# An expert's first weight matrix: its magnitude from ScalarE's sums of squares instead of VectorE's largest absolute values

## The chip, the core and the metric

The kernel runs on one core of a Trainium2 chip. The metric is the device time of one launch in microseconds (us), the median of three runs. The engines named below are PE (TensorE, the matmuls), PEld (its weight loads), DVE (VectorE), ACT (ScalarE), POOL (GpSimd) and SP (SyncE, which here only issues transfers).

## The reference, cut to what matters

Attention through 32 packed queries gives x, 4608 tokens of 512 numbers. A mixture of eight experts with top-1 routing follows, then a dense layer. All is float32.

```python
expert_idx = np.argmax(x @ w_gate, axis=1)
for e in range(E):                          # E = 8, w1: 512 x 1024, w2: 1024 x 512
    xe = x[expert_idx == e]
    h = np.maximum(xe @ w1[e], 0.0)
    out[expert_idx == e] = gate_w * (h @ w2[e])
...
h = out @ w_in                              # 512 x 2048
r = np.maximum(h, 0.0)
return (s * (r * r) + b) @ w_out            # 2048 x 512
```

## The kernel before

The kernel sorts the tokens by expert into tiles of 128 tokens. Attention and the first expert tiles come first. From tile 11 on (`FIRST`) the expert tiles and the dense layer are interleaved, and that is the stage that this text is about: tiles 11 to 38, from about 325 us to 1215 us of the span. After it the dense layer runs alone.

In that stage a float32 operand is split into two float16 parts, high and low, and a product is made of three matmuls (high by high, low by high, high by low). To split the weights of a tile, `wscale` finds one scale for the whole matrix, and `wsplit` writes the high part with ACT (`wh`, L885) and the low part with DVE (`wl`, L887), in four chunks of 128 x 1024. Part 0 is the first matrix w1, part 1 the second one w2. The scale needs a magnitude of the matrix, which is found chunk by chunk: for part 0 by `big1`, a DVE reduction of the largest absolute value (L845), for part 1 by `big2`, an ACT square whose sum goes to an accumulator (L854). `wscale` then takes the largest of the four (L860), exchanges it between the partitions on POOL (L862), and works the scale out in a few tiny DVE instructions.

`slot(i, ...)` is one step of the stage. An even slot (tile 11, 13, ...) runs the eight column blocks of the dense layer's first product (`mlp_1`, four before and four after the second product of the previous tile, `moe_2s`), and then the first product of its own tile (`moe_1s`). An odd slot has the two halves of the dense layer's second product (`mlp_2`) in their place. Two slots thus handle two expert tiles and 256 tokens of the dense layer.

The preparation of weights stands in one queue of generators, `wq`, in the order scale, split, load of the next tile's part, magnitude of the next part: `wscale(i,0)`, `wsplit(i,0)`, `wload(i+1,0)`, `big2(i)`, `wscale(i,1)`, `wsplit(i,1)`, `wload(i+1,1)`, `big1(i+1)`. `tick(n)`, called between groups of matmuls, takes the next n steps from `wq` and then one step of each chain in `chains` (`xsplit` for the tokens of the next tile, `moe_y` for the results of the last, `gate`). Each engine works through its own instructions in the order in which the program issues them, so an instruction of `wq` that waits holds up all that its engine has behind it. All the magnitudes of part 0 of tiles 12 to 38 fall into odd slots.

`wload` issues four transfers of 512 KB on SP, each conditional on a change of expert (`chg`), and each after the split of the old contents of its chunk. `xsplit` ends with a transposing transfer on the same SP queue, `xTs`, which `moe_1s` of the tile reads. In `mlp_1`, ACT frees a block of PSUM (`r`, L976); there are two such blocks (`gp`), so the third group of matmuls waits for the first one's `r`.

Of the kernel before, what the change touches and what calls it, by code (L numbers as in the profile page):

```python
# [11 lines left out]
F32 = mybir.dt.float32  # L12
F16 = mybir.dt.float16
I32 = mybir.dt.int32
BF16 = mybir.dt.bfloat16
AF = mybir.ActivationFunctionType
ALU = mybir.AluOpType
AX = mybir.AxisListType
# [3 lines left out]
FIRST = 11  # L22
# [85 lines left out]
SURE = NMT - 4  # L108
# [38 lines left out]
def attn_moe_mlp_kernel(ctx, tc, q, k, v, p, w_gate, w1, w2, w_in, w_out, s_, b_, cst_d, csh_d, out):  # L147
    nc = tc.nc
    V, A, T, G, SY = nc.vector, nc.scalar, nc.tensor, nc.gpsimd, nc.sync
# [5 lines left out]
    def flat(t):  # L155
        return t.rearrange("p a b -> p (a b)")
# [23 lines left out]
    st = {}  # L180
# [3 lines left out]
    wf = [[wp.tile([128, 4, 256], F32, name=f"wf1{c}") for c in range(4)],  # L184
          [wp.tile([128, 2, 512], F32, name=f"wf2{c}") for c in range(4)]]

    def wload(i, part):
        src = (w1, w2)[part]
        if part == 0:
            st["er", i] = (SY.value_load(eid[0:1, i:i + 1], min_val=0, max_val=E - 1),  # L190
                           SY.value_load(chg[0:1, i:i + 1], min_val=0, max_val=1) if i else None)
        e, ch = st["er", i]
        sl, cond = src[ds(e, 1)].rearrange("o c p f -> (o c) p f"), dict(cond=ch) if i else {}
        for c in range(4):
            SY.dma_start(out=flat(wf[part][c]), in_=sl[c], **cond)

    io = ctx.enter_context(tc.tile_pool(name="io", bufs=2))
# [328 lines left out]
    def gather(i):  # L526
        x = io.tile([128, XW], F32, tag="x", name="xg", bufs=3)
        G.indirect_dma_start(out=x, out_offset=None, in_=xd if i >= EARLY else xd[0:128 * KNOWN, :], in_offset=bass.IndirectOffsetOnAxis(ap=rho[:, i:i + 1] if i >= EARLY else rho0[:, i:i + 1], axis=0))
        st["x", i] = x

    def moe_x(i, ps):
        x = st["x", i]
        st["xp", i] = pt = ps.tile([128, 4, 128], F32, tag="t", name="ptx")
        for c in range(4):
            T.transpose(pt[:, c, :], x[:, 128 * c:128 * c + 128], ident)

    def moe_xc(i):
        xT = io.tile([128, 4, 128], F32, tag="xT", name="xT")
        A.copy(out=xT, in_=st.pop(("xp", i)))
        st["xT", i] = xT  # L540

    def gate(i):

        lg = st["x", i][:, DM:DM + E]
        nm = io.tile([128, 1], F32, tag="nm", name="nm")
        V.tensor_reduce(out=nm, in_=lg, axis=AX.X, op=ALU.max, negate=True)
        yield
        ex = io.tile([128, E], F32, tag="ex", name="ex")
        f = io.tile([128, 1], F32, tag="f", name="f")
        A.activation(out=ex, in_=lg, func=AF.Exp, bias=nm, accum_out=f)  # L550
        st["f", i] = f
# [252 lines left out]
    io2 = ctx.enter_context(tc.tile_pool(name="io2", bufs=2))  # L804
# [6 lines left out]
    def moe_1(i):  # L811
        xT = st.pop(("xT", i))
        hT = io.tile([128, 8, 128], F32, tag="hT", name="hT")
        for c in range(4):
            if c % 2 == 0:
                hp = ps_h.tile([128, 4, 128], F32, tag="h", name="hp")
            for m in range(2):
                for kk in range(4):
                    T.matmul(hp[:, 2 * (c % 2) + m, :], wf[0][c][:, kk, 128 * m:128 * m + 128], xT[:, kk, :], start=kk == 0, stop=kk == 3)
            if c % 2:  # L820
                A.activation(out=hT[:, 2 * c - 2:2 * c + 2, :], in_=hp, func=AF.Relu)
            tick(FW[0])
        st["hT", i] = hT
# [12 lines left out]
    def pow2(s, a, mul):  # L836
        V.tensor_scalar(out=s, in0=a, scalar1=1e-30, scalar2=mul, op0=ALU.max, op1=ALU.mult)
        V.tensor_scalar(out=s.bitcast(I32), in0=s.bitcast(I32), scalar1=0x7F800000, scalar2=None, op0=ALU.bitwise_and)

    def big1(i):  # L840

        am = io.tile([128, 4], F32, tag="am1", name="am1")
        st["am1", i] = am
        for c in range(4):
            V.tensor_reduce(out=am[:, c:c + 1], in_=wf[0][c], axis=AX.XY, op=ALU.max, apply_absolute_value=True)  # L845
            yield

    def big2(i):

        am = mp.tile([128, 4], F32, tag="am2", name="am2")  # L850
        st["am2", i] = am
        for c in range(4):
            jk = mp.tile([128, 2, 512], F16, tag="jk2", name="jk2", bufs=1)
            A.activation(out=jk, in_=wf[1][c], func=AF.Square, accum_out=am[:, c:c + 1])  # L854
            yield

    def wscale(i, part):
        am = st.pop((f"am{part + 1}", i))
        m = mp.tile([128, 1], F32, tag=f"wm{part}", name="wm")
        V.tensor_reduce(out=m, in_=am, axis=AX.X, op=ALU.max)  # L860
        pm = mp.tile([128, 1], F32, tag=f"wp{part}", name="wp")
        G.partition_all_reduce(pm, m, 128, bass_isa.ReduceOp.max)  # L862
        yield
        s = mp.tile([128, 1], F32, tag=f"ws{part}", name="ws")
        r = mp.tile([128, 1], F32, tag=f"wr{part}", name="wr")
        if part == 0:
            pow2(s, pm, 0.25)
            V.reciprocal(out=r, in_=s)  # L868
        else:
            V.tensor_scalar(out=s, in0=pm, scalar1=1e-30, scalar2=None, op0=ALU.max)  # L870
            V.tensor_scalar(out=s.bitcast(I32), in0=s.bitcast(I32), scalar1=1, scalar2=0x7F800000,
                            op0=ALU.logical_shift_right, op1=ALU.bitwise_and)
            V.reciprocal(out=r, in_=s)
            V.tensor_scalar(out=r, in0=r, scalar1=2.0 ** -54, scalar2=None, op0=ALU.mult)
            s1 = st["ws", i]
            V.tensor_scalar(out=s, in0=s, scalar1=2.0 ** 54, scalar2=s1, op0=ALU.mult, op1=ALU.mult)
        st["ws", i] = s
        st["wr", i, part] = r
        yield
# [59 lines left out]
    def mlp_load(k):  # L939

        yT = io2.tile([128, 2, 4, 256], F16, tag="yT", name="yT")
        rows = ybuf[256 * k:256 * k + 256, :]
        SY.dma_start_transpose(out=yT.rearrange("p a c t -> p (a c) t"), in_=rows[:, 0:DM].bitcast(F16))
        st["yT", k] = yT
        y = io2.tile([128, 2, 2], F32, tag="yg", name="yg")
        SY.dma_start(out=y, in_=rows[:, DM:DM + 2].rearrange("(t p) c -> p t c", p=128))
        st["y", k] = y

    def mlp_y(k):
        ys = []  # L950
        y = st.pop(("y", k))
        for t in range(2):
            dt = io.tile([128, 1], F32, tag="dt", name="dt", bufs=4)
            V.tensor_tensor(out=dt, in0=y[:, t, 0:1], in1=y[:, t, 0:1], op=ALU.mult)
            tk_ = io.tile([128, 1], I32, tag="tk", name="tk", bufs=4)
            V.tensor_copy(out=tk_, in_=y[:, t, 1:2].bitcast(I32))
            ys.append((dt, tk_))
        st["ys", k] = ys
# [44 lines left out]
    wq = []  # L1003
# [23 lines left out]
    for i in range(1, FIRST):  # L1027
        if i == 1:
            wq.append(cg)
            chains.append(gate(1))  # L1030
        elif i + 1 < FIRST:
            moe_x(i + 1, ps_tr)
            moe_xc(i + 1)
        if i > 1:
            gather(i + 2)
        if i == FIRST - 1:
            mlp_load(0)
        moe_1(i)
        wload(i + 1, 0)
        if i == FIRST - 1:  # L1040
            mlp_y(0)
            chains.append(xsplit(FIRST))
            wq.append(big1(FIRST))
        if i == 1:
            gather(3)
            moe_x(2, ps_tr)
            moe_xc(2)
        moe_2(i)
        wload(i + 1, 1)
        chains.append(gate(i + 1))  # L1050
# [9 lines left out]
                    op0=ALU.logical_shift_right, op1=ALU.bitwise_and)  # L1060
    V.tensor_scalar(out=qm[:, 8:9].bitcast(I32), in0=top[:, 1:2].bitcast(I32), scalar1=1, scalar2=0x7F800000,
                    op0=ALU.logical_shift_right, op1=ALU.bitwise_and)
# [13 lines left out]
    mp = ctx.enter_context(tc.tile_pool(name="mp", bufs=2, side="right"))  # L1076
# [3 lines left out]
    def later(f, *a):  # L1080
        f(*a)
        return
        yield
# [13 lines left out]
    done = {}  # L1097
    i = FIRST
# [17 lines left out]
    def queue1(i):  # L1116
        if i < SURE:
            done[i, 0] = wsplit(i, 0)
            wq.extend([wscale(i, 0), done[i, 0]] + ([later(wload, i + 1, 0)] if i + 1 < SURE else []) + [big2(i)])

    def queue2(i):
        if i < SURE:
            done[i, 1] = wsplit(i, 1)
            wq.extend([wscale(i, 1), done[i, 1]])
            if i + 1 < SURE:
                wq.extend([later(wload, i + 1, 1), big1(i + 1)])

    def slot(i, x1, x2):

# [92 lines left out]
```

## Time and profile before

| what | before |
|---|---|
| median of three runs | 1397.02 us (1391.12 to 1397.62) |
| the profiled execution's own time | 1395.76 us |
| its span, first to last instruction | 1394.0 us |
| PE, PEld busy | 1350.3 us (97%), 934.8 us (67%) |
| DVE, ACT, POOL busy | 1055.7 us (76%), 798.8 us (57%), 187.1 us (13%) |
| mean granted clock of TensorE | 0.992 |

The profile is of one execution. Its own time is 1.8 us above its span, which is what lies around the first and the last instruction. A busy time is a sum over the instructions of an engine; matmuls are pipelined and overlap. An idle time in brackets stands with the engine or transfer that ended it.

### The profile page before, as it was taken

Reading aid. Unit: us, or ns where it says so; the run is one execution under the profiler, and the core shown is the slowest. Engines: PE = TensorE matmul, PEld = TensorE weight load, DVE = VectorE, ACT = ScalarE, POOL = GpSimd, SP = SyncE. Lnnn points to the kernel's source line nnn. Section 1 sums busy time; section 2 is a strip of 40 time slices with the busy share of each in tenths; the row PEclk is TensorE's granted clock in tenths of the full one; section 3 lists DMA queues with packets and bytes.
Section 4 is the critical chain, followed back from the end, with each engine's and each line's share of the span. In section 5 each row is a group of like instructions: output and inputs, shape, how many; then the busy total and the mean of one; then the engine's idle time right before and its main releaser. Section 6 shows DMA issues by size and latency. Waiting matters only on the chain. (4 is left out here: it accounts for less than half of the span.)

```text
span 1394.0 us, 29467 instructions
## 1 busy us (share of the span) xinstructions
PE 1350.3 (97%) x11365; PEld 934.8 (67%) x11365; DVE 1055.7 (76%) x2330; ACT 798.8 (57%) x1314; POOL 187.1 (13%) x283
## 2 busy tenths in 40 slices
PE   7999989999999999999999999899999999999998
PEld 4666766677575857667675857576676858667764
DVE  3777888887798788888888888788888888733322
ACT  3655444455675757677675757577676757523221
POOL 0223211111011010111111110101111110100000
PEclk9999999999999999999999999999999999999999
DMA  9897347462116111141223211611112111111000
GB/s 331 277 364 257 131 173 265 147 204 58 27 40 164 44 40 39 44 155 44 55 92 107 48 45 39 160 35 47 32 48 53 32 46 47 31 27 40 16 16 16
DMA packets 106145, 133.62 MB, mean 96 GB/s; under 512 B 77135, under 2 KB 79311, under 8 KB 102928
## 3 DMA queue, kind: packets, MB, share of 16 engines
q1 hardware_dynamic: 91696, 92.76, 22.6%
q0 software_dynamic: 9120, 29.32, 6.4%
q10 hardware_dynamic: 5184, 9.61, 1.9%
q8 instruction: 91, 1.49, 0.5%
q14 instruction: 54, 0.44, 0.1%
HBM read 216.39 MB, written 29.30 MB: 176 GB/s over the span
## 5 line engine op out<-in xcount | busy, mean ns | idle before, releaser
L971 PE MATMUL gp<-yT,win_h 128*128 128x256 f16 x1152 | 314.6, 273 | 3.6 <-ACT r L976 3.4
L973 PE MATMUL gp<-yT,win_l 128*128 128x256 f16 x1152 | 314.6, 273 | 0.0
L972 PE MATMUL gp<-yT,win_h 128*128 128x256 f16 x1152 | 314.6, 273 | 0.0
L887 DVE SCALAR_TENSOR_TENSOR wl<-wf,wr,wh 128x1024 f16<-128x1024 f32 x224 | 278.3, 1279 | 23.9 <-ACT wh L885 23.8
L885 ACT ACTIVATE wh<-wf,wr 128x1024 f16<-128x1024 f32 x224 | 245.8, 1139 | 59.9 <-DVE wr L868 45.0
L993 PE MATMUL op<-wout_h,g 128*128 128x512 f16 x512 | 194.0, 379 | 0.8 <-DVE osb L999 0.8
L994 PE MATMUL op<-wout_l,g 128*128 128x512 f16 x512 | 194.0, 379 | 0.0
L995 PE MATMUL op<-wout_h,g 128*128 128x512 f16 x512 | 194.0, 379 | 0.0
L976 ACT ACTIVATE r<-gp,cf 128x512 f32<-128x512 f32 x144 | 98.8, 686 | 141.5 <-PE gp L973 141.5
L979 DVE TENSOR_TENSOR r<-r 128x512 f32<-128x512 f32 x144 | 99.7, 692 | 81.1 <-ACT g L978 57.3
L919 PE MATMUL hps<-xTs,wh 128*128 128x128 f16 x896 | 154.4, 221 | 6.1 <-DMA xTs<-xs 5.9
L920 PE MATMUL hps<-xTs,wh 128*128 128x128 f16 x896 | 154.4, 221 | 0.0
L921 PE MATMUL hps<-xTs,wl 128*128 128x128 f16 x896 | 154.4, 221 | 0.0
L845 DVE TENSOR_REDUCE am<-wf 128x1 f32<-128x1024 f32 x112 | 132.0, 1211 | 0.0
L972 PEld LDWEIGHTS <-win_h 128*128 128x128 f16 x1152 | 112.9, 98 | 18.3 <-issue 3.6
L971 PEld LDWEIGHTS <-win_h 128*128 128x128 f16 x1152 | 112.9, 98 | 17.7 <-issue 3.0
L973 PEld LDWEIGHTS <-win_l 128*128 128x128 f16 x1152 | 112.9, 98 | 13.3
L854 ACT ACTIVATE jk<-wf 128x1024 f16<-128x1024 f32 x112 | 118.1, 1054 | 2.6
L924 ACT ACTIVATE hTs<-hps 128x512 f16<-128x512 f32 x56 | 33.4, 597 | 122.0 <-PE hps L921 122.0
L919 PEld LDWEIGHTS <-wh 128*128 128x128 f16 x896 | 88.7, 99 | 9.0 <-issue 6.8
L980 DVE TENSOR_TENSOR g<-r,g 128x512 f16<-128x512 f32 x128 | 88.6, 692 | 4.4
L995 PEld LDWEIGHTS <-g 128*128 128x128 f16 x512 | 50.1, 98 | 60.4
(254 smaller groups left out, 2326.2 us busy)
## 6 DMA issues: line engine op xcount, KB each, us to landing
wf<-in_moe_w_dram SPq DMA_DIRECT2D x304, 512.0 KB
xd<-x ACTq DMA_DIRECT2D x36, 260.5 KB
k<-in_k_dram SPq DMA_DIRECT2D x16, 576.0 KB
v<-in_v_dram SPq DMA_DIRECT2D x16, 512.0 KB
q<-in_q_dram SPq DMA_DIRECT2D x8, 1024.0 KB
raw<-in_moe_w_in_dram SPq DMA_DIRECT2D x8, 1024.0 KB
raw<-in_moe_w_out_dram SPq DMA_DIRECT2D x8, 1024.0 KB
p<-in_p_dram SPq DMA_DIRECT2D x8, 128.0 KB
```

The lines of the kernel that those rows point to most:

```text
L845: V.tensor_reduce(out=am[:, c:c + 1], in_=wf[0][c], axis=AX.XY, op=ALU.max, apply_absolute_value=True)
L885: A.activation(out=wh[part][c], in_=wf[part][c], func=AF.Copy, scale=r)
L887: V.scalar_tensor_tensor(out=wl[part][c - 1], in0=wf[part][c - 1], scalar=r, in1=wh[part][c - 1], op0=ALU.mult, op1=ALU.subtract)
L919: T.matmul(o, h_, xT[:, 0, kk, :], start=kk == 0, stop=False)
L920: T.matmul(o, h_, xT[:, 1, kk, :], start=False, stop=False)
L921: T.matmul(o, l_, xT[:, 0, kk, :], start=False, stop=kk == 3)
L971: T.matmul(hp[:, i, :], h_, yT[:, 0, kk, :], start=kk == 0, stop=False)
L972: T.matmul(hp[:, i, :], h_, yT[:, 1, kk, :], start=False, stop=False)
L973: T.matmul(hp[:, i, :], l_, yT[:, 0, kk, :], start=False, stop=kk == 3)
L993: T.matmul(op, h_, wout_h[:, kf, :], start=kf == 0, stop=False)
L994: T.matmul(op, h_, wout_l[:, kf, :], start=False, stop=False)
L995: T.matmul(op, l_, wout_h[:, kf, :], start=False, stop=kf == 15)
```

## The change

`big1` and `big2` become one function `big(i, part)`, which squares a chunk on ACT and sums it into an accumulator for either part. The 112 DVE reductions of part 0 (28 tiles of four chunks) go, and 112 ACT squares with their accumulator reads come in, at the same places in `wq`. In `wscale`, part 0 gets the form of part 1: five tiny DVE instructions where there were three. The small tiles `am` and the thrown-away squares (`jkw`, one buffer for both parts) come from the pool `io2`, which exists before the first call; `am1`, `am2` and `jk2` go.

```diff
-    def big1(i):
-        am = io.tile([128, 4], F32, tag="am1", name="am1")
-        st["am1", i] = am
+    def big(i, part):
+        am = io2.tile([128, 4], F32, tag=f"am{part}", name="am")
+        st["am", i, part] = am
         for c in range(4):
-            V.tensor_reduce(out=am[:, c:c + 1], in_=wf[0][c], axis=AX.XY, op=ALU.max, apply_absolute_value=True)
+            jk = io2.tile([128, 1024], F16, tag="jkw", name="jkw", bufs=1)
+            A.activation(out=jk, in_=flat(wf[part][c]), func=AF.Square, accum_out=am[:, c:c + 1])
             yield
-    def big2(i):
-        am = mp.tile([128, 4], F32, tag="am2", name="am2")
...
-            jk = mp.tile([128, 2, 512], F16, tag="jk2", name="jk2", bufs=1)
-            A.activation(out=jk, in_=wf[1][c], func=AF.Square, accum_out=am[:, c:c + 1])
...
     def wscale(i, part):
-        am = st.pop((f"am{part + 1}", i))
+        am = st.pop(("am", i, part))
...
+        up = 2.0 ** (54 if part else 59)
+        V.tensor_scalar(out=s, in0=pm, scalar1=1e-30, scalar2=None, op0=ALU.max)
+        V.tensor_scalar(out=s.bitcast(I32), in0=s.bitcast(I32), scalar1=1, scalar2=0x7F800000,
+                        op0=ALU.logical_shift_right, op1=ALU.bitwise_and)
+        V.reciprocal(out=r, in_=s)
+        V.tensor_scalar(out=r, in0=r, scalar1=1.0 / up, scalar2=None, op0=ALU.mult)
         if part == 0:
-            pow2(s, pm, 0.25)
-            V.reciprocal(out=r, in_=s)
+            V.tensor_scalar(out=s, in0=s, scalar1=up, scalar2=None, op0=ALU.mult)
         else:
...
+            V.tensor_scalar(out=s, in0=s, scalar1=up, scalar2=st["ws", i], op0=ALU.mult, op1=ALU.mult)
...
-            wq.append(big1(FIRST))
+            wq.append(big(FIRST, 0))
...
-... + [big2(i)])
+... + [big(i, 1)])
...
-                wq.extend([later(wload, i + 1, 1), big1(i + 1)])
+                wq.extend([later(wload, i + 1, 1), big(i + 1, 0)])
```

## Rows read from the trace of the kernel before

**Rows 1.** Page, part 1: busy us, share of the span, instructions.

```profile
PE 1350.3 (97%) x11365; PEld 934.8 (67%) x11365; DVE 1055.7 (76%) x2330; ACT 798.8 (57%) x1314; POOL 187.1 (13%) x283
```

**Rows 2.** What PE waited for from 300 us on: total us, times, longest.

```profile
PE hps L919 <- DMA xTs<-xs: 5.9, 2, 3.8
PE gp L971 <- ACT r L976: 3.4, 1, 3.4
PE tp L1056 <- DVE dg L738: 1.8, 1, 1.8
```

**Rows 3.** Busy us (count) by engine, granted clock, DMA share, GB/s, per stretch.

```profile
456.00:888.00 432.00, 432.00 (x3590) 298.56 (x3589) 369.42 (x716) 297.70 (x444) 56.36 (x68) 1.00 0.25 66
...
394.00:396.00 2.00, 0.67 (x4) 0.47 (x4) 1.63 (x6) 1.97 (x4) 0.00 (x0) 0.64 0.00 0
396.00:398.00 2.00, 2.00 (x11) 1.40 (x10) 1.97 (x3) 1.97 (x3) 0.00 (x0) 0.51 0.00 0
...
430.00:432.00 2.00, 2.00 (x11) 0.93 (x10) 0.75 (x3) 1.61 (x2) 0.00 (x0) 1.00 0.00 0
```

**Rows 4.** ACT timeline: first hidden activation of five even slots; start, length, idle.

```profile
417.76 0.60 ACT L924 ACTIVATE hTs<-hps 128x512 f16<-128x512 f32 x1 [1.33 <-PE hps L921]
...
484.42 0.60 ACT L924 ACTIVATE hTs<-hps 128x512 f16<-128x512 f32 x1 [1.32 <-PE hps L921]
...
547.18 0.60 ACT L924 ACTIVATE hTs<-hps 128x512 f16<-128x512 f32 x1 [1.33 <-PE hps L921]
...
860.98 0.60 ACT L924 ACTIVATE hTs<-hps 128x512 f16<-128x512 f32 x1 [1.33 <-PE hps L921]
...
929.09 0.60 ACT L924 ACTIVATE hTs<-hps 128x512 f16<-128x512 f32 x1 [1.33 <-PE hps L921]
```

**Rows 5.** Page, part 5: both forms of magnitude; busy us, mean ns.

```profile
L845 DVE TENSOR_REDUCE am<-wf 128x1 f32<-128x1024 f32 x112 | 132.0, 1211 | 0.0
...
L854 ACT ACTIVATE jk<-wf 128x1024 f16<-128x1024 f32 x112 | 118.1, 1054 | 2.6
```

**Rows 6.** DVE timeline of an odd slot: start, length, idle before.

```profile
423.31 2.34 DVE L845 TENSOR_REDUCE am<-wf 128x1 f32<-128x1024 f32 x2
...
429.09 0.16 DVE L860 TENSOR_REDUCE wm<-am 128x1 f32<-128x4 f32 x1
...
439.28 0.16 DVE L860 TENSOR_REDUCE wm<-am 128x1 f32<-128x4 f32 x1 [0.77 <-ACT jk L854]
```

**Rows 7.** ACT timeline of the same odd slot.

```profile
420.93 1.14 ACT L885 ACTIVATE wh<-wf,wr 128x1024 f16<-128x1024 f32 x1
...
430.39 4.27 ACT L885 ACTIVATE wh<-wf,wr 128x1024 f16<-128x1024 f32 x4 [2.81 <-DVE wr L868]
434.56 1.05 ACT L854 ACTIVATE jk<-wf 128x1024 f16<-128x1024 f32 x1
...
440.77 4.27 ACT L885 ACTIVATE wh<-wf,wr 128x1024 f16<-128x1024 f32 x4 [0.94 <-DVE wr L874]
```

**Rows 8.** SP's queue in the same odd slot: issue start, time issuing.

```profile
432.88 0.36 SPq L195 DMA_DIRECT2D wf<-in_moe_w_dram  x1
...
438.23 1.28 SPq L906 DMA_TRANSPOSE xTs<-xs  x1
```

**Rows 9.** ACT timeline where an odd slot goes over into an even one.

```profile
578.44 0.60 ACT L924 ACTIVATE hTs<-hps 128x512 f16<-128x512 f32 x1 [3.12 <-PE hps L921]
582.32 0.60 ACT L924 ACTIVATE hTs<-hps 128x512 f16<-128x512 f32 x1 [3.28 <-PE hps L921]
583.74 0.69 ACT L976 ACTIVATE r<-gp,cf 128x512 f32<-128x512 f32 x1 [0.82 <-PE gp L973]
```

**Rows 10.** ACT timeline of tile 12's odd slot and the even slot behind it.

```profile
369.08 4.27 ACT L885 ACTIVATE wh<-wf,wr 128x1024 f16<-128x1024 f32 x4 [8.40 <-DVE wr L868]
...
393.98 0.72 ACT L900 ACTIVATE xs<-xg,xr 128x512 f16<-128x512 f32 x1 [5.92 <-DVE xr L897]
394.61 0.67 ACT L976 ACTIVATE r<-gp,cf 128x512 f32<-128x512 f32 x1
```

More of the change, by code (lines that the diff above doesn't have):

```diff
@@ L838, in pow2 @@
         V.tensor_scalar(out=s.bitcast(I32), in0=s.bitcast(I32), scalar1=0x7F800000, scalar2=None, op0=ALU.bitwise_and)
-    def big1(i):
-        am = io.tile([128, 4], F32, tag="am1", name="am1")
-        st["am1", i] = am
+    def big(i, part):
+        am = io2.tile([128, 4], F32, tag=f"am{part}", name="am")
+        st["am", i, part] = am
         for c in range(4):
-            V.tensor_reduce(out=am[:, c:c + 1], in_=wf[0][c], axis=AX.XY, op=ALU.max, apply_absolute_value=True)
-            yield
-    def big2(i):
-        am = mp.tile([128, 4], F32, tag="am2", name="am2")
-        st["am2", i] = am
-        for c in range(4):
-            jk = mp.tile([128, 2, 512], F16, tag="jk2", name="jk2", bufs=1)
-            A.activation(out=jk, in_=wf[1][c], func=AF.Square, accum_out=am[:, c:c + 1])
+            jk = io2.tile([128, 1024], F16, tag="jkw", name="jkw", bufs=1)
+            A.activation(out=jk, in_=flat(wf[part][c]), func=AF.Square, accum_out=am[:, c:c + 1])
             yield
     def wscale(i, part):
-        am = st.pop((f"am{part + 1}", i))
+        am = st.pop(("am", i, part))
         m = mp.tile([128, 1], F32, tag=f"wm{part}", name="wm")
@@ L865, in wscale @@
         r = mp.tile([128, 1], F32, tag=f"wr{part}", name="wr")
+        up = 2.0 ** (54 if part else 59)
[4 more added lines that the diff above has]
+        V.tensor_scalar(out=r, in0=r, scalar1=1.0 / up, scalar2=None, op0=ALU.mult)
         if part == 0:
-            pow2(s, pm, 0.25)
-            V.reciprocal(out=r, in_=s)
-        else:
[L870 to L876, printed above, removed]
+            V.tensor_scalar(out=s, in0=s, scalar1=up, scalar2=None, op0=ALU.mult)
+        else:
+            V.tensor_scalar(out=s, in0=s, scalar1=up, scalar2=st["ws", i], op0=ALU.mult, op1=ALU.mult)
         st["ws", i] = s
@@ L1118, in queue1 @@
             done[i, 0] = wsplit(i, 0)
-            wq.extend([wscale(i, 0), done[i, 0]] + ([later(wload, i + 1, 0)] if i + 1 < SURE else []) + [big2(i)])
+            wq.extend([wscale(i, 0), done[i, 0]] + ([later(wload, i + 1, 0)] if i + 1 < SURE else []) + [big(i, 1)])
     def queue2(i):
```

## The prediction

> **What bounds the kernel now.** The page's first part comes first [rows 1]: PE is busy for 97% of the span, DVE for 76%, ACT for 57%. A busy PE says little by itself, so the next view is what PE waited for from 300 us on [rows 2]: twice a transposed token tile `xTs` (5.9 us, of which one wait is 3.8), once an ACT result `r` (3.4 us), once a DVE result before the stage begins (1.8 us). Then the stretches [rows 3], whose columns behind the length are PE, PEld, DVE, ACT and POOL: from 456 to 888 us PE is busy for all of 432 us at full clock, DVE for 369 and ACT for 298. The last check is the rhythm [rows 4]: the same instruction of an even slot comes at 484.42 and at 547.18, so an undisturbed pair of slots takes 62.76 us, with no wait of PE in it.
>
> So neither DVE nor ACT is the bound in an undisturbed pair. Moving work between them is worth nothing there, as long as ACT doesn't become late. What is to be had is in the three disturbed places, and these cost more than their waits. From 417.76 to 484.42 are 66.66 us, 3.90 more than a pair, for a wait of 2.1 (5.9 less 3.8). From 860.98 to 929.09 are 68.11, 5.35 more, for a wait of 3.8. The third place, the wait for `r` near 394, shows why: behind it the granted clock is 0.64 and 0.51 for two stretches of 2 us [rows 3], that is, in part the lower of its two levels, 1.2 GHz in place of 2.4. PE had idled for 3.4 us before it fell. In these stretches 0.67 us of work at 0.64 and 2.00 us at 0.51 lose 0.24 + 0.98 = 1.2 us, so this place costs 3.4 + 1.2 = 4.6 us.
>
> The Trainium skill (Trainium Kernel Development and Optimization, the paragraph on reading a trace under Performance Expectations) says that matmul busy time misjudges how near a kernel is to its limit and that weight-load busy time is one of the better measures. By that rule PE, with loads busy for 67%, could have room of up to a third, and freeing DVE would pay in every pair. The constant 62.76 us without a wait shows no such room that a faster DVE could fill.
>
> **What goes and comes, in instructions.** 112 reductions of 1.211 us leave DVE, and 112 squares of 1.054 us come to ACT [rows 5]. The busy sum of DVE falls by 132 us, that of ACT rises by 118 us and 112 accumulator reads. Off the path this is free.
>
> ScalarE: Activation LUTs, Rules for kernel authors, in the Trainium skill, speaks against the move: maxima and products belong on VectorE, which it calls up to about three times as fast per element in 16 bit. By that rule a chunk on ACT would cost up to 3 x 1.21 = 3.6 us; the trace disagrees for these float32 chunks, with 1.05 against 1.21. I go by the rows.
>
> **The odd slot.** Here the reductions stand between the end of one split and the start of the next, and they are in series with it. In the slot around 430 us [rows 6, 7], ACT ends the last high part of w2 at 420.93 + 1.14 = 422.07. DVE ends its low part and starts reducing at 423.31, the token chain `xsplit` comes between the reductions, and the largest of the four is taken at 429.09. ACT starts the next split at 430.39, after an idle 2.81.
>
> After the change ACT can square at once from 422.07. What four squares with their reads cost up to the same reduction is seen with part 1 (w2) of the same slot: from 434.56 to 439.28, 4.72 us. So the reduction comes at 426.79. From there to the split's start were 1.30 us for part 0 (429.09 to 430.39); with the longer `wscale` it is what part 1 needs, 439.28 to 440.77, 1.49 us. The split starts at 428.28 in place of 430.39, 2.1 us sooner, and all that hangs on it in this slot comes sooner too: low parts, loads, `xTs`, the second magnitude, the second split. The two more tiny instructions are in this sum (0.19 us). The POOL exchange is unchanged. The squares need w1 loaded, as the reductions did, and these never waited for it (idle 0.0 [rows 5]); behind a square that did wait, ACT's hidden activations and every `r` would be queued.
>
> **The three places.**
> *Near 448.* `xTs` is issued at 438.23 behind four loads of w1, the first of them at 432.88, and each of these waits for a low part of the split [rows 8]. The transfer engines are idle just before (share 0.00 from 430 to 432 [rows 3]), so the whole train should move 2.1 us forward. The wait is 2.1 us. I take it as gone, clock loss and all: 3.9 us. Bounds: 0, if the transposing transfer is held up by something that doesn't move, and 3.9.
> *Near 893.* Same train, wait 3.8 us, so 1.7 remain, and I let the clock loss stay: a gain of 2.1 us. Bounds: 0, and 5.35 - 1.7 = 3.7 if the shorter wait no longer lowers the clock.
> *Near 394.* Tile 12's split starts at 369.08, after ACT idled 8.40 us for the DVE scale, and the lag runs on: ACT is held at `xs` until 393.98 (idle 5.92, on DVE's `xr`), `r` comes only at 394.61, and PE stands [rows 10]. DVE is late because it does the last two reductions before `xr`. In the new kernel the split starts 2.1 us sooner, ACT does the next four squares where it idled 5.92, and DVE comes to `xr` without reductions. The late `r` ended at 394.61 + 0.67 = 395.28, and PE had waited 3.4 us, so it is needed by 391.9. What brings it forward is 2.1 us of the earlier split, and of the rest of the 5.92 that ACT idled for `xr` some two reductions of 1.21, which DVE no longer has in front of it: 2.1 + 2.4 = 4.5 us, against 3.4 needed, while the squares take 4.72 of ACT, which fit into the 5.92. No wait, but a margin of a microsecond or less. I take the full 4.6 us; bounds 0 and 4.6.
> *Near 324* (1.8 us [rows 2]): DVE's queue is shorter by four reductions, but `xs` comes behind four squares on ACT, and 4.72 us there stand against 4 x 1.21 = 4.84 on DVE. I take 0; bounds 1.8 gained, 0.2 lost.
>
> Sum: 4.6 + 3.9 + 2.1 = 10.6 us. From the profiled execution's own 1395.76 this gives 1385.2; that execution is 1.26 us under the median of the runs, so the median should be **1386.4 us**.
>
> **Rivals.**
> *The transfers don't move.* Both waits for `xTs` stay, and only the place at 394 goes: 1397.0 - 4.6 = 1392.4 us. For it: the train is 2 MB and shares the engines with gathers that don't move. Against it: the idle engines before it. If the place at 394 stays as well, because its margin fails, nothing is left: 1397 us.
> *ACT becomes the bound (the other side).* The seam from an odd to an even slot is the place: four squares must fit before the first `r`, or PE, with two blocks of PSUM, stops at the third group. ACT's idle time there is 3.12 + 3.28 + 0.82 = 7.22 us [rows 9] against 4.72 of squares. So it decides from 7.22 us on at the earliest, half as much again as the rows show, or if the squares must come at the wrong moments of that idle time. Each microsecond over that point costs some 13 seams 13 us, and the clock loss of 1.2 us each with it: 1397 - 10.6 + 13 x 2.2 = 1415 us. The rows speak against it. By the rule of the ScalarE page in the Trainium skill four squares would take 14.5 us, 7.3 beyond that point, and the kernel would be some 13 x (7.3 + 1.2) = 110 us slower; it has no more than 1 in 100 here.
> *PE had hidden room.* Every pair would shorten, beyond the waits: all places gone makes 4.6 + 3.9 + 5.35 + 1.8 = 15.7 us, 1381 us, and anything below that needs a pair under 62.76.
>
> **How the numbers follow.** The forecast has 0.60, its own range is 1381 to 1391 (between 6 and 16 us gained). The transfers that don't move have 0.18, nothing gained 0.11, ACT as bound 0.08, hidden room 0.03. About 0.5% (7 us, so 1390 and 1404) is what a measurement of this kernel can tell from no change; the runs of before spread over 6.5 us. Faster: nearly all of the forecast and the hidden room, 0.61. Slower: 0.08. Same: 0.31. The range leaves out the hidden room, most of ACT as bound and a tail of nothing gained: 1380 to 1398.
>
> **What would show it.** Right: 224 squares and no reduction at L845's place; ACT's sum up by about 140 us, DVE's down by about 130; the split of part 0 in odd slots 2.1 us nearer to the split before it (6.2 after its end in place of 8.3); no wait of PE for `r` near 394; the wait near 448 gone and that near 893 halved; pairs still 62.76 us. Wrong: ACT idle at none of the seams and PE waiting for `r` in many pairs (ACT is the bound), the split sooner but the two waits for `xTs` as long (transfers), or pairs of another length (hidden room). What would most likely break the sum is the margin near 394 and the landing near 448, where tenths decide whether the clock falls.

## The result, and the profile after

The changed kernel takes 1380.12 us (median of four runs, 1375.91 to 1381.62) against 1397.32 us for the kernel before (four runs): a ratio of 0.9887, interval 0.9864 to 0.991. A second comparison of the same kernel gave 1380.71 us against 1392.15, ratio 0.9915 (0.9901 to 0.993). The ratios here and below come from all the runs of both sides; they are not the quotient of the two medians and can differ from it by 0.1 to 0.2%. The change is faster by about 1%. The profiled execution took 1381.62 us, with a span of 1379.8, 14.2 us less than before.

The busy times of the page, and the one form of magnitude that is left (busy us, mean ns of one):

```profile
PE 1344.1 (97%) x11365; PEld 930.5 (67%) x11365; DVE 939.2 (68%) x2274; ACT 918.5 (67%) x1538; POOL 187.0 (14%) x283
...
L846 ACT ACTIVATE jkw<-wf 128x1024 f16<-128x1024 f32 x224 | 235.7, 1052 | 5.0 <-DMA wf<-in_moe_w_dram 0.6
```

DVE lost 117 us and ACT gained 120 [rows 1]; both are now busy for about two thirds of the span. What PE waited for from 300 us on [rows 2]:

```profile
PE hps L911 <- DMA xTs<-xs: 1.9, 1, 1.9
PE tp L1048 <- DVE dg L738: 1.2, 1, 1.2
PE op L985 <- DVE osb L991: 0.8, 1, 0.8
```

The wait for `r` is gone, and of the two waits for `xTs` one is left, of 1.9 us. The markers of the even slots, as in [rows 4] (ACT timeline; start, length, idle before):

```profile
347.12 0.60 ACT L916 ACTIVATE hTs<-hps 128x512 f16<-128x512 f32 x1 [1.33 <-PE hps L913]
...
410.79 0.60 ACT L916 ACTIVATE hTs<-hps 128x512 f16<-128x512 f32 x1 [1.33 <-PE hps L913]
...
473.55 0.60 ACT L916 ACTIVATE hTs<-hps 128x512 f16<-128x512 f32 x1 [1.33 <-PE hps L913]
...
536.31 0.60 ACT L916 ACTIVATE hTs<-hps 128x512 f16<-128x512 f32 x1 [1.33 <-PE hps L913]
...
850.11 0.60 ACT L916 ACTIVATE hTs<-hps 128x512 f16<-128x512 f32 x1 [1.33 <-PE hps L913]
...
914.91 0.60 ACT L916 ACTIVATE hTs<-hps 128x512 f16<-128x512 f32 x1 [1.33 <-PE hps L913]
```

From 410.79 to 473.55 are 62.76 us, where 66.66 were before: an undisturbed pair. The undisturbed pair itself, 473.55 to 536.31, is still 62.76 us. From 850.11 to 914.91 are 64.80 us in place of 68.11. These intervals are the measure used below, since they hold one place each. Tile 11 to 13, which holds the place near 394, is 63.67 (347.12 to 410.79) in place of 68.91, from the marker of tile 11 before the change to 417.76:

```profile
348.85 0.60 ACT L924 ACTIVATE hTs<-hps 128x512 f16<-128x512 f32 x1 [1.33 <-PE hps L921]
```

Where the time came from, by these intervals: 5.24 us near 394, 3.90 near 448, 3.31 near 893, together 12.45 us. The remaining 1.73 us of the two spans lie ahead of tile 11's marker (348.85 before, 347.12 after). Other executions put that marker at 345.2 to 348.7 us where tile 11 is squared on ACT (once) and at 345.8 to 352.1 where it is not, so these 1.7 us can't be put down to the change.

### The profile page after: what moved, and what is told of

Read it like the earlier page. It is cut to its first block, busy times and chain, and to the rows that moved or that the text cites. A ratio compares the mean times of both kernels' runs of the same rounds, so it can differ in the third digit from the quotient of the medians.

```text
span 1379.8 us, 29799 instructions
## 1 busy us (share of the span) xinstructions
PE 1344.1 (97%) x11365; PEld 930.5 (67%) x11365; DVE 939.2 (68%) x2274; ACT 918.5 (67%) x1538; POOL 187.0 (14%) x283
## 5 line engine op out<-in xcount | busy, mean ns | idle before, releaser
L846 ACT ACTIVATE jkw<-wf 128x1024 f16<-128x1024 f32 x224 | 235.7, 1052 | 5.0 <-DMA wf<-in_moe_w_dram 0.6
L911 PE MATMUL hps<-xTs,wh 128*128 128x128 f16 x896 | 151.5, 219 | 1.9 <-DMA xTs<-xs 1.9
L913 PE MATMUL hps<-xTs,wl 128*128 128x128 f16 x896 | 151.5, 219 | 0.0
L912 PE MATMUL hps<-xTs,wh 128*128 128x128 f16 x896 | 151.5, 219 | 0.0
L987 PEld LDWEIGHTS <-g 128*128 128x128 f16 x512 | 50.1, 98 | 60.4
L986 PEld LDWEIGHTS <-g 128*128 128x128 f16 x512 | 50.1, 98 | 59.9 <-issue 1.5
```

What stands on the lines that cost most here:

```text
L846: A.activation(out=jk, in_=flat(wf[part][c]), func=AF.Square, accum_out=am[:, c:c + 1])
L911: T.matmul(o, h_, xT[:, 0, kk, :], start=kk == 0, stop=False)
L912: T.matmul(o, h_, xT[:, 1, kk, :], start=False, stop=False)
L913: T.matmul(o, l_, xT[:, 0, kk, :], start=False, stop=kk == 3)
L986: T.matmul(op, h_, wout_l[:, kf, :], start=False, stop=False)
L987: T.matmul(op, l_, wout_h[:, kf, :], start=False, stop=kf == 15)
```

## The experiments

"Places" and "load" name two theories. "Places": the moved reductions stood in series ahead of three waits of PE, and only these matter. "Load": the gain comes from taking work off DVE. Each interval below is from the marker of an even slot to that of the next, in one profiled execution; the steady value is 62.76 us, and 63.67 for tile 11 to 13, which has extra work. The three columns hold the places near 394, 448 and 893 us, in this order.

| kernel | squared on ACT | tile 11 to 13 | 13 to 15 | 27 to 29 | ratio to before (interval) |
|---|---|---|---|---|---|
| before | none | 68.91 | 66.66 | 68.11 | |
| after | all | 63.67 | 62.76 | 64.80 | 0.9887 (0.9864 to 0.991) |
| after, again | all | 63.67 | 62.76 | 62.76 | 0.9915 (0.9901 to 0.993) |
| `e_none` | none | 69.28 | 64.62 | 67.38 | 1.0004 (0.9986 to 1.0023) |
| `e_four` | 12, 13, 14, 28 | 63.68 | 62.75 | 63.70 | 0.9917 (0.9899 to 0.9935) |
| `e_rest` | all but these four | 67.64 | 67.84 | 64.81 | 0.9987 (0.9968 to 1.0006) |
| `e_t12_13` | 12, 13 | 63.68 | 64.10 | 68.25 | 0.9959 (0.9939 to 0.9978) |
| `e_t14_28` | 14, 28 | 69.09 | 62.76 | 63.85 | 0.9957 (0.9934 to 0.998) |
| `e_t12` | 12 | 65.24 | 62.76 | 64.17 | one run, no interval |
| `e_t13` | 13 | 65.29 | 64.92 | 67.73 | one run, no interval |
| `e_xts_before` | none | 69.28 | 62.76 | 62.76 | 0.9943 (0.9921 to 0.9964) |
| `e_xts_after` | all | 63.68 | 62.76 | 62.76 | 0.9905 (0.9872 to 0.9939) |

### Which tiles carry the gain

The changed kernel, with a choice by tile of where part 0's magnitude is found; a tile that is not in the list gets the old reduction and the old three-instruction scale.

```diff
+            if part or i in SQ:
                 A.activation(out=jk, in_=flat(wf[part][c]), func=AF.Square, accum_out=am[:, c:c + 1])
+            else:
+                V.tensor_reduce(out=am[:, c:c + 1], in_=wf[0][c], axis=AX.XY, op=ALU.max, apply_absolute_value=True)
```

No tile (`SQ` empty):

> The changed kernel's pools and code, but every part-0 magnitude stays a DVE reduction with the three-instruction scale. Theory 'places' (the gain comes from moved reductions that stood in series ahead of three waits of PE: tiles 12 and 13 near 394 us, tile 14 near 448, tile 28 near 893): no change, 1397 us, all three waits still there. Theory 'load' (the gain comes from DVE's busy sum): no change, 1397 us. Theory 'form' (it comes from the other pools): near the changed kernel, 1380 us.

It took 1392.94 us beside 1393.98 of before, and all three waits are there. So the other pools and the rest of the new code make no difference that the runs can tell.

Four tiles:

> Only tiles 12, 13, 14 and 28 are squared on ACT, 16 of 112 chunks; all others stay DVE reductions. Theory 'places': the pair intervals shrink as in the changed kernel, by 5.2 + 3.9 + 3.3 us, so some 1385 us. Theory 'load': 16/112 of the 17 us, 2.5 us, so 1395 us.

It took 1381.93 us beside 1393.98. With 16 of 112 chunks moved, the gain is 12 us. What PE waited for from 300 us on:

```profile
PE tp L1056 <- DVE dg L739: 1.9, 1, 1.9
PE op L993 <- DVE osb L999: 0.8, 1, 0.8
PE hps L919 <- DMA xTs<-xs: 0.8, 1, 0.8
```

The other 24 tiles:

> The complement: tiles 12, 13, 14 and 28 stay DVE reductions, the other 24 tiles (96 of 112 chunks) are squared on ACT. Theory 'places': the waits near 394, 448 and 893 stay, at most the 1.7 us ahead of the first tile go: 1395 to 1397 us. Theory 'load': 96/112 of the 17 us: 1382.5 us.

It took 1391.84 us beside 1393.98, a difference that the interval does not tell from none. With 96 of 112 chunks moved, the waits stay:

```profile
PE hps L919 <- DMA xTs<-xs: 3.9, 2, 3.3
PE gp L971 <- ACT r L976: 3.0, 1, 3.0
PE hps L919 <- ACT jkw L848: 1.9, 1, 1.9
```

"Load" falls with these two. One line is not as "places" had it: near 893 the wait of 1.9 us is ascribed to an ACT square, not to `xTs`, and the interval there is 64.81, not 68. The waiting product does not read that square's result, and SP issues `xTs` as late as before (880.11 us, 20.48 behind the marker at 859.63; before 881.45 - 860.98 = 20.47). So it is most likely the tokens again, landing sooner in this execution; that is not shown.

The two pairs of tiles by themselves:

> Only tiles 12 and 13 are squared on ACT (8 of 112 chunks). Theory 'places': the wait for r near 394 goes with its clock loss, 5.2 us (the pair from the first even slot's hidden activation to the next shrinks from 68.9 to 63.7), and the two waits for the transposed tokens stay: ratio about 0.996. Theory 'load': 8/112 of the gain, nothing that can be seen.

> Only tiles 14 and 28 are squared on ACT (8 of 112 chunks). Theory 'places': the wait near 448 goes (3.9 us) and that near 893 halves (3.3 us), the wait for r near 394 stays: ratio about 0.995. Theory 'load': nothing that can be seen.

They took 1387.03 and 1388.76 us beside 1394.78. Each cures its own places and leaves the others (table). The two gains, 0.41% and 0.43%, add up to what the four tiles give, 0.83%, though each is known only to about 0.2%.

### The two parts of the cure near 394

> Only tile 12 is squared on ACT: the split of tile 12 comes some 2.1 us sooner (the prediction's first part of the cure near 394), and the two reductions in front of xr stay. The wait for r, 3.4 us before, should be about 1.3 us. Rival: that part alone is enough, no wait.

> Only tile 13 is squared on ACT: the split of tile 12 is as late as before, but DVE comes to xr without reductions (the prediction's second part, 2.4 us). The wait for r should be about 1 us. Rival: ACT, with four more squares in a late slot, is later than before, and the wait is 3.4 us or more.

They took 1384.97 and 1393.28 us in one run each. PE's wait for `r` was 1.4 us with tile 12 alone and 1.1 us with tile 13 alone, against 3.4 with neither and none with both. The ACT timeline of the first, then of the second:

```profile
367.29 4.26 ACT L885 ACTIVATE wh<-wf,wr 128x1024 f16<-128x1024 f32 x4 [1.44 <-DVE wr L869]
...
392.18 0.72 ACT L900 ACTIVATE xs<-xg,xr 128x512 f16<-128x512 f32 x1 [3.91 <-DVE xr L897]
392.81 0.67 ACT L976 ACTIVATE r<-gp,cf 128x512 f32<-128x512 f32 x1
```

```profile
372.32 4.26 ACT L885 ACTIVATE wh<-wf,wr 128x1024 f16<-128x1024 f32 x4 [8.40 <-DVE wr L876]
...
394.39 0.72 ACT L900 ACTIVATE xs<-xg,xr 128x512 f16<-128x512 f32 x1 [0.15 <-DVE xr L897]
395.02 0.67 ACT L976 ACTIVATE r<-gp,cf 128x512 f32<-128x512 f32 x1
```

With tile 12 alone the split starts early (367.29, 17.8 us after the marker of tile 11 in place of 20.2), but ACT still idles 3.91 us for `xr`. With tile 13 alone the split is as late as before, idle 8.40 as in [rows 10], but `xr` no longer holds ACT up (0.15 us). The first takes 2.0 us off the wait and the second 2.3, where the prediction had 2.1 and 2.4.

### The transposing transfer ahead of the loads

One more step of the chains ahead of the second product makes SP issue `xTs` before the four loads of w1 in an odd slot. On the other engines the order of the work stays.

```diff
             flush(done[i - 1, 1])
+            tick(0)
             moe_2s(i - 1)
```

In the kernel before:

> The kernel before with one more step of the chains ahead of the second product of the previous tile, so that SP issues the transposing transfer of an odd slot ahead of the four loads of w1 and not behind them; no other engine's instructions change. Theory 'places' (the tokens are late only because their transfer stands behind loads that wait for the split): both waits for them go, 3.9 + 5.35 us, the wait for r near 394 stays: ratio about 0.993. Rival: the transfer is held up by traffic that stays (gathers, the other loads): the waits stay, ratio 1.00.

It took 1385.61 us beside 1394.78. SP's queue in the odd slot around 430 us, to be held against [rows 8]:

```profile
433.55 1.26 SPq L906 DMA_TRANSPOSE xTs<-xs  x1
436.90 10.16 SPq L195 DMA_DIRECT2D wf<-in_moe_w_dram  x8
```

The transfer now goes out at 433.55, right behind the low token part that it reads. That is 15.9 us after the even slot's marker (417.65) in place of 20.5, so 4.6 us earlier. What PE waited for from 300 us on:

```profile
PE gp L971 <- ACT r L976: 3.8, 1, 3.8
PE tp L1056 <- DVE dg L738: 2.6, 1, 2.6
PE op L993 <- DVE osb L999: 0.8, 1, 0.8
```

Both waits for `xTs` are gone, without any square moved; that for `r` is not. So the tokens were late because their transfer stood behind the four loads in SP's queue, and those wait for the split [rows 8].

In the changed kernel:

> The same step in the changed kernel. Theory 'places': the remaining wait near 893 (1.9 us) goes, nothing else changes: 2 us less than the changed kernel, ratio about 0.987 to the kernel before. Rival: no change against the changed kernel.

No wait for `xTs` is left, and the stage runs at 62.76 us throughout. Beside the changed kernel on one chip:

> The changed kernel again, beside the next one on the same chip. The spans of the two profiles lay 14.2 us apart, the medians of four runs each 17.2: by theory 'places' the markers in the trace give 12.4 us for the three places and 1.7 ahead of the stage, so about 14 us, ratio 0.990.

> The changed kernel with the transposing transfer issued ahead of the loads of w1, again: 2 us less than the changed kernel beside it (0.15%), which may be too little to be told apart.

The medians were 1380.71 and 1378.26 us beside 1392.15, both ratios 0.9915 (the second one's interval 0.9892 to 0.9937). The two can't be told apart: in that execution of the changed kernel the wait near 893 was not there either. The waits for `xTs` differ from one execution to the next (with the old order and tiles 14 and 28 on DVE from none to 3.3 us near 448 and from 1.3 to 3.8 near 893; with both on ACT none near 448 and from none to 1.9 near 893), and in the three profiled executions with the new order there is none. Whether the new order is worth anything on top of the squares, the times do not show.

### The point from which ACT would be the bound

The changed kernel with every square of part 0 done twice. This is added work; no value changes.

```diff
+            for _ in range(1 if part else 2):
                 A.activation(out=jk, in_=flat(wf[part][c]), func=AF.Square, accum_out=am[:, c:c + 1])
```

> The changed kernel with each part-0 square done twice (added work, same values): a batch of four costs ACT 9.4 us in place of 4.72. The prediction's point of 7.22 us of ACT idle time at a seam is passed by 2.2 us: by it each of 13 seams costs 2.2 us, with the clock loss 3.4 us, and the three places come back (12 us): 1380 + 12 + 29 to 44 = 1421 to 1436 us. Rival: r may be late until PE has filled the second block, some 2 us more, so the seams cost nothing yet and only the three places come back: some 1392 to 1397 us.

It took 1432.52 us beside 1393.98, ratio 1.0265 (1.0235 to 1.0295). One pair in the ACT timeline:

```profile
560.88 0.60 ACT L917 ACTIVATE hTs<-hps 128x512 f16<-128x512 f32 x1 [1.12 <-PE hps L914]
...
595.99 0.58 ACT L917 ACTIVATE hTs<-hps 128x512 f16<-128x512 f32 x1
...
601.39 0.67 ACT L969 ACTIVATE r<-gp,cf 128x512 f32<-128x512 f32 x1
...
625.89 0.60 ACT L917 ACTIVATE hTs<-hps 128x512 f16<-128x512 f32 x1 [1.12 <-PE hps L914]
```

The pair takes 625.89 - 560.88 = 65.01 us, 2.25 more than 62.76, and ten of the thirteen pairs are that long. ACT comes to the odd slot's hidden activations (595.99 and 598.69) without any idle time, and the first `r` of the even slot starts behind the last square. PE's waits in the same pair, 1.9 of the 2.25 us:

```profile
PE gp L964 <- ACT r L969: 1.1, 1, 1.1
PE op L986 <- DVE osb L992: 0.8, 1, 0.8
```

The second wait is not at the seam. It is the odd slot's second half of `mlp_2`, which waits for DVE to take the first half (`osb`), and DVE does that behind the split, which the slot's own four doubled squares hold up (DVE timeline):

```profile
574.53 0.16 DVE L853 TENSOR_REDUCE wm<-am 128x1 f32<-128x4 f32 x1 [6.85 <-ACT jkw L847]
...
579.06 0.75 DVE L992 SCALAR_TENSOR_TENSOR osb<-op,dt,bcs 128x512 f32<-128x512 f32 x1
```

So a pair loses what the point of 7.22 us gives (9.44 - 7.22 = 2.2 us), but by luck: the seam costs only 1.1 us of it, half of what was expected there, and 0.8 us comes from a place that was not in the sum. The fall of the clock, which the expectation's upper end charged at each seam, does not appear in these pairs; from 500 to 900 us the granted clock is 1.00 in each stretch of 50 us. The rest of the loss sits in the three places, whose intervals are 74.63, 68.98 and 69.96 us, and about 5 us ahead of them, where PE's wait near 324 was 6.0 us in place of 1.2.

## Why the prediction was right

*The bound.* Neither DVE nor ACT sets the pace of an undisturbed pair: pairs stayed at 62.76 us with none, some or all of the squares moved, that is, up to 117 us less of DVE and 120 more of ACT. PE is busy all through such a pair [rows 3]. The rule of the Trainium skill (Trainium Kernel Development and Optimization, the paragraph on reading a trace under Performance Expectations) made a hidden reserve of PE a rival; no run shows one that the freed DVE filled, although weight loads are busy for 67% of the span before and after.

*The odd slot.* The forecast was that ACT squares at once and that the split starts 2.1 us sooner. ACT and DVE in the odd slot after the change, to be held against [rows 6, 7]:

```profile
413.96 1.14 ACT L877 ACTIVATE wh<-wf,wr 128x1024 f16<-128x1024 f32 x1
415.00 1.04 ACT L846 ACTIVATE jkw<-wf 128x1024 f16<-128x1024 f32 x1
...
421.19 4.27 ACT L877 ACTIVATE wh<-wf,wr 128x1024 f16<-128x1024 f32 x4 [0.90 <-DVE wr L864]
```

```profile
415.14 1.28 DVE L879 SCALAR_TENSOR_TENSOR wl<-wf,wr,wh 128x1024 f16<-128x1024 f32 x1 [0.22 <-ACT wh L877]
...
419.71 0.16 DVE L852 TENSOR_REDUCE wm<-am 128x1 f32<-128x4 f32 x1 [2.12 <-ACT jkw L846]
```

The squares follow the high part directly (415.00). The largest of the four is taken 4.71 us later (4.72 predicted), the split starts 6.09 us after the end of the last split's ACT part at 413.96 + 1.14 (6.21 predicted, 8.32 before). `xTs` is issued sooner too:

```profile
429.04 1.28 SPq L898 DMA_TRANSPOSE xTs<-xs  x1
```

That is 18.25 us after the even slot's marker, against 20.47 before (438.23 - 417.76 [rows 4, 8]): 2.2 us.

So the gain in the slot comes from the order of the work and not from a faster instruction. The prediction set 1.05 us on ACT against 1.21 on DVE, but the accumulator read goes with each square: four squares take 4.72 us, 1.18 each, and DVE's reductions follow each other after 1.17 (2.34 for two [rows 6]). In series the two forms cost about the same. What is saved is the time in which DVE wrote its low part and ran the token chain before the last reduction.

*Near 448*, 3.9 us predicted, 3.90 measured. *Near 394*, 4.6 predicted, 5.24 measured: the mechanism and its two halves were right, and the size was 0.6 us short. The clock loss of 1.2 us was not the error. PE in the place before the change:

```profile
378.54 0.22 PE L919 MATMUL hps<-xTs,wh 128*128 128x128 f16 x1 [0.23 <-ACT jk L561]
...
395.33 0.37 PE L971 MATMUL gp<-yT,win_h 128*128 128x256 f16 x1 [3.41 <-ACT r L976]
395.50 0.42 PE L972 MATMUL gp<-yT,win_h 128*128 128x256 f16 x1
...
397.84 0.34 PE L971 MATMUL gp<-yT,win_h 128*128 128x256 f16 x1
398.02 0.27 PE L972 MATMUL gp<-yT,win_h 128*128 128x256 f16 x1
```

Behind the wait twelve matmuls come 0.21 us apart (395.50 to 398.02) and the next ones 0.11, a loss of 1.2 us. What the prediction left out is a second wait of 0.23 us in the same interval. The last 0.4 us are not accounted for, though each of the shorter waits, too, cost 0.1 to 0.2 us more than its length. The rows of the place after the change:

```profile
364.95 4.27 ACT L877 ACTIVATE wh<-wf,wr 128x1024 f16<-128x1024 f32 x4 [1.44 <-DVE wr L864]
...
385.53 0.68 ACT L968 ACTIVATE r<-gp,cf 128x512 f32<-128x512 f32 x1
...
387.03 0.72 ACT L892 ACTIVATE xs<-xg,xr 128x512 f16<-128x512 f32 x1 [0.15 <-DVE xr L889]
387.65 0.67 ACT L968 ACTIVATE r<-gp,cf 128x512 f32<-128x512 f32 x1
```

ACT idles 0.15 us for `xr` where it idled 5.92, and the second `r` comes 40.5 us after the marker of tile 11 in place of 45.8. *Near 893*, 2.1 predicted, 3.31 measured, 1.9 us of wait left as forecast (1.7). The term was mis-sized because I let the clock loss stay. It did not; the stretches around the wait (PE, PEld, DVE, ACT, POOL busy, granted clock):

```profile
878.00:880.00 2.00, 0.65 (x4) 0.10 (x1) 1.01 (x5) 0.23 (x2) 1.18 (x2) 1.00 0.35 104
880.00:882.00 2.00, 1.47 (x27) 1.50 (x28) 0.00 (x0) 0.00 (x0) 0.68 (x1) 1.00 1.00 393
```

The clock is 1.00 before and behind it, so the wait costs 64.80 - 62.76 = 2.04 us, hardly more than itself. The prediction had this as the upper bound of the term, 3.7. In the second profiled execution of the changed kernel the wait is absent and the interval is 62.76, so the size of this term also depends on the execution. *Near 324*, taken as nothing: the wait is 1.2 us in one execution of the changed kernel and 2.0 in another, against 1.8 before and 2.7 in `e_none`; it varies without the change.

*The sum*, 10.6 us, against 12.45 by the intervals, 11.4 by the medians of the second comparison and 17.2 by those of the first, which has four runs on each side. The first comparison's 1380.12 us is outside the forecast's own range of 1381 to 1391 and inside the wider one, 1380 to 1398, by 0.1 us; that is luck. The prediction also held that less than 1381 needs a pair under 62.76, and no pair is shorter. What the three places do not explain of the 17.2 us is open, and the second comparison does not show it again.

*The busy sums* moved less than the signs had it: ACT by 120 us in place of about 140, DVE by 117 in place of about 130. In part, instructions overlap: an accumulator read starts 0.1 us before its square ends. The rest was not followed up.

*The rival on ACT* failed for the reason given. At a seam the squares lie in ACT's idle time, and what is left of it is still there:

```profile
567.57 0.60 ACT L916 ACTIVATE hTs<-hps 128x512 f16<-128x512 f32 x1 [3.15 <-PE hps L913]
...
570.25 0.60 ACT L916 ACTIVATE hTs<-hps 128x512 f16<-128x512 f32 x1 [1.05 <-PE hps L913]
...
572.87 0.69 ACT L968 ACTIVATE r<-gp,cf 128x512 f32<-128x512 f32 x1 [0.99 <-PE gp L965]
```

From 3.12 + 3.28 + 0.82 us [rows 9] it went to 3.15 + 1.05 + 0.99: the first two squares stand before this stretch, one in each gap within it, and `r` still waits for PE. The doubled squares then showed that the rival is real once more work comes to ACT: the seam lost 1.1 us with 9.44 us of squares. Where exactly it begins is not shown. The rule of the ScalarE page in the Trainium skill (ScalarE: Activation LUTs, Rules for kernel authors) would have put these operations on VectorE; its factor of three is for 16 bit. The trace does not bear it out for these float32 chunks, which cost 1.18 us on ACT and 1.17 on DVE, and the kernel is 1% faster with them on ACT.

## What to carry to other kernels

When the engine that sets the pace is already full in the undisturbed stretches, moving work between two others pays only where the moved work stands in series ahead of one of the bound engine's few waits: here 16 of 112 chunks carried the whole gain, as far as the runs can tell. Find these places by the length of a repeating interval, not by busy sums, and price them with the clock that can fall behind them. Work out how much idle time the receiving engine has at its tightest seam, and what else stands behind the moved work, because a wait that comes up there is paid at every repetition.

## What the hardware showed that was not expected

The same kernel's transfers land differently from one execution to the next: the wait near 893 was 1.9 us in one execution of the changed kernel and absent in another. With tile 28 on DVE it was 3.8 us in the kernel before, 3.1 in `e_none` and 1.3 in `e_t12`, whose code is the same there.

Behind the wait of 3.4 us near 394 the granted clock fell to about the lower of its two levels, and the interval lost 1.8 us on top of the wait, 1.2 of them by the clock. Behind the waits that the changes had shortened, 1.9 us near 893 and 1.4 us in `e_t12`, the intervals lost 0.2 us on top. There, shortening a wait paid more than its length. But the length alone does not decide. In the kernel before, a wait of 2.1 us near 448 was followed by a clock of 0.50 (450 to 452 us) and lost 1.8 us on top. In `e_rest`, after a wait of 3.0 us for `r` near 394, the clock stayed at 1.00 (columns as in [rows 3]; the wait ends at 394.07):

```profile
394.00:396.00 2.00, 1.93 (x18) 1.73 (x18) 1.64 (x6) 1.97 (x4) 0.00 (x0) 1.00 0.00 0
```

Its interval of 67.64 us is 4.0 over 63.67, hardly more than its two waits of PE, 3.0 and 0.6 us.

Before the change the second hidden activation of an odd slot came 3.88 us after the first [rows 9], where one half of the product takes 2.68; after the change it comes after 2.68 everywhere in the steady stretch. What held it up before is open; PE did not wait for it.
